# A chunked scan before a mixture of experts: own products head by head, and the decay product in the rows' bank

## The chip, the cores and the metric

The kernel runs on one NeuronCore of a Trainium2 chip. The metric is device time in microseconds: the median of 3 runs is 271.99 us (271.18 to 272.0). One more execution, the profiled one, took 271.81 us; its span, from the first to the last recorded instruction, is 270.0 us. Engines are called PE (TensorE), DVE (VectorE), ACT (ScalarE), POOL (GpSimd) and SP (the queue that issues most DMAs).

## The reference, cut to what matters

Two parts follow each other. The first is a state-space scan (Mamba2 SSD) over 4 batches, 8 heads and 768 steps, with 32 values per head and a state of 16 x 32. It goes chunk by chunk:

```
CB = C_chunk @ B_chunk.T                      # scores of a chunk
y_intra = (CB * L) @ x_chunk                  # L: decay from step j to step i, causal
y_inter = (C_chunk @ state) * decay_to_i      # what came before the chunk
state = decay_full * state + sum_j decay_from_j * outer(B_j, x_j)
```

The second is a top-1 mixture of 8 experts over the 3072 rows of 256 values that the scan makes: a gate product gives 8 logits per row, the row goes to its largest, passes `relu(x @ w1[e]) @ w2[e]` (256 to 1024 to 256) and is scaled by its softmax weight.

## The kernel before

**Tiling of the scan.** The chunk is 64 steps here. The eight heads and two batches of a pair stand side by side: the 128 partitions are two sequences of 64 steps each, a second index `s` holds the other half, and `NT` = 24 chunk pairs (2 pairs of batches, `NC` = 12 chunks each) are walked in order. A loop `for n in range(0, NT + 2)` (L801) is a pipeline written out by hand, three chunks deep: `n` is the chunk whose decays and scores are made, `k = n - 1` the one whose state and output are made, `j = k - 1` the one whose output is turned into rows. All of it stands under a manual schedule: each engine executes its instructions in the order in which the Python code emits them, and the framework adds the semaphore waits between engines. [...]

**One iteration before the change.** `decay(n)` (L355) makes L for all eight heads with one scan on DVE. `fade(k)` (L409) multiplies the carried state by its decay, two ACT instructions, into `Sd`. `own(k)` (L393) forms the chunk's own contribution to the state, B^T x, in PSUM bank A: eight products of two heads of B (32 columns) with two heads of x (64 columns), each in two passes of fp32, so 16 matmuls. A product of two heads with two heads also holds the two cross terms, which aren't wanted. `decay_in` (L329) makes the decay factors of chunk n+2 with three full-size bf16 matmuls into columns 128 to 255 of the same bank A, and ACT copies them to `dec` (L339). `rank_pe` runs in some iterations (below). `state(k)` (L419) adds own products and `Sd`; as the cross terms have to be masked, it takes one DVE instruction per head of the pair, each with the mask column `par[:, u]` as its scalar. `y(k)` (L435) makes the output: first the state products (`ctd` with the carried state S, 32*64 tiles of the array), then the products of M with x (64*32 tiles), into one PSUM tile; ACT copies it to `yT`.

Then come `scores(n)` (L369, the tile `g`, 32*64 tiles), `scaled_B(n)` (L363, on POOL, `bs` = B times L's last column), `decayed_C([n + 2])` (L341, on POOL, `ctd` = C times `dec`), `a_rows(n + 1)` (L348, one bf16 matmul that makes the next scan's input `abc`) and `weigh(n)` (L383, on DVE, M = g times L). ACT has `masks` (the tile `ctm`) in iterations with n mod 4 of 1 or 2, and single jobs at n = 3, 5, 6, 7, 10 and 12. `rows(j)` (L463) turns the output of chunk j into rows of 256 values and 8 logits with two products of 128x136 (four matmuls) in a PSUM bank with the tag "rows", and ACT copies them out (L470). All matmuls of the scan go through the helper `mm` (L175), so the profile shows them with line 176; they are told apart by their tiles. `mm` also counts passes and sends the next loads from SP when a count is reached.

**Routing.** The rows come in groups (`RGS`). When a group is complete, `due` lists three stages for later iterations: stage 0 `choose_max` (maximum, subtraction and comparison, on DVE), stage 1 `choose` (the one-hot row `oh_all`, on DVE, then counts on POOL) and stage 2 `rank_pe` and `rank` (four to six small matmuls, then two DVE instructions that make the position `pos`). Before the change stages 0 and 1 fall into the same iteration for all but the first group, and stage 2 into the one after; the rank's PSUM tile has the tag "rows". After stage 2 each iteration places one chunk's rows in DRAM with an indirect DMA from POOL (L553). At n = 23 the first expert's rows are loaded from DRAM (`a_load`), and the experts follow, with PE products `h_ps` (L685) and `y_ps` (L720).

Of the kernel before, what the change touches and what calls it, by code (L numbers as in the profile page):

```python
# [9 lines left out]
FP32 = mybir.dt.float32  # L10
# [4 lines left out]
ALU = mybir.AluOpType  # L15
# [4 lines left out]
NB, NH, S, D, NS = 4, 8, 768, 32, 16  # L20
N, DM, E, F = 3072, 256, 8, 1024
CH = 64
NP = NB // 2
NC = S // CH
NT = NP * NC
CG = 4
# [3 lines left out]
R0 = [sum(RGS[:i]) for i in range(len(RGS))]  # L30
RG = max(RGS)
# [13 lines left out]
def ssd_then_moe(ctx, tc, x, ad_in, az_in, B, BT, CT, w_gate, w1, w2, out):  # L45
# [16 lines left out]
    def bc(ap, shape):  # L62
        return ap.to_broadcast(shape)
# [17 lines left out]
    azp = [sm.tile([128, 512], BF16, name=f"azp{p}") for p in range(NP)]  # L81
    hsel = sm.tile([128, NC, NH, NS], BF16, name="hsel")
    adp = [sm.tile([128, NP * 128], BF16, name=f"adp{i}") for i in range(3)]
    bs = [sm.tile([128, 8, NS], FP32, name=f"bs{i}") for i in range(2)]

    oh_all = route.tile([128, NT, E], BF16, name="oh_all")
    cnt = route.tile([128, len(RGS) + 2, E], BF16, name="cnt")
# [216 lines left out]
    def decay_ready(p, t):  # L304
        r = slice(2 * p, 2 * p + 2)
        clip(nc.gpsimd, t[:, r])
        nc.gpsimd.tensor_copy(d1[:, r, 0:1], t[:, r, 0:1])
        nc.gpsimd.memset(t[:, r, 0:1], 0.0)
# [14 lines left out]
    def state_bank(k):  # L323

        if "A" not in st[k]:
            st[k]["A"] = ps.tile([128, 2, 128], FP32, name="A", bufs=1)
        return st[k]["A"]

    def decay_in(ns, bank):  # L329
        for i, n in enumerate(ns):  # L330
# [32 lines left out]
    def scaled_B(n):  # L363
        if n % NC == NC - 1:
            return
        nc.gpsimd.tensor_tensor(out=bs[n % 2], in0=gr[n // CG]["B"][:, n % CG].rearrange("p (h m) -> p h m", h=8),  # L366
                                in1=bc(st[n]["L"][:, :, CH - 1:CH], [128, 8, NS]), op=ALU.mult)

    def scores(n):  # L369
        c = n % CG  # L370
# [22 lines left out]
    def own(k):  # L393
        if k % NC == NC - 1:
            return
        A = state_bank(k)
        xk = gr[k // CG]["x"][:, k % CG]

        for s in range(2):
            for t in range(2):  # L400
                for v in range(2):
                    r = slice(64 * t, 64 * t + 64)
                    h = 4 * s + 2 * v
                    mm(A[32 * (2 * t + v):32 * (2 * t + v) + 32, 0, 64 * s:64 * s + 64],
                                     lhsT=bs[k % 2][r, h:h + 2].rearrange("p u m -> p (u m)"),
                                     rhs=xk[r, h * D:(h + 2) * D], start=(s == 0), stop=(s == 1),
                                     skip_group_check=True)

    def fade(k):  # L409

# [8 lines left out]
    def state(k):  # L419
        c = k % NC  # L420
        if c == NC - 1:
            return
        new = wk.tile([128, 2, 2 * D], FP32, name="S", bufs=3)
        A = st[k]["A"][:, 0].rearrange("p (s d) -> p s d", s=2)
        for u in range(2):
            d = slice(D * u, D * u + D)
            if c == 0:
                nc.vector.tensor_scalar(out=new[:, :, d], in0=A[:, :, d], scalar1=par[:, u:u + 1], scalar2=None,
                                        op0=ALU.mult)
            else:  # L430
                nc.vector.scalar_tensor_tensor(out=new[:, :, d], in0=A[:, :, d], scalar=par[:, u:u + 1],  # L431
                                               in1=st[k]["Sd"][:, :, d], op0=ALU.mult, op1=ALU.add)
        carry[k + 1] = new

    def y(k):  # L435
        p = ps.tile([128, 2, 512], FP32, name="y", bufs=1)
        inter = k % NC > 0
        xk = gr[k // CG]["x"][:, k % CG]
        if inter:
            for s in range(2):  # L440
                for t in range(2):
                    for v in range(2):
                        r = slice(64 * t + 32 * v, 64 * t + 32 * v + 32)
                        o = s * CH
                        mm(p[64 * v:64 * v + 64, t, s * CH:s * CH + CH], lhsT=carry[k][r, s],
                                         rhs=st[k]["ctd"][r, o:o + CH], start=(s == 0), stop=False,
                                         skip_group_check=True)
        for s in range(2):
            for q in range(4):
                for t in range(2):  # L450
                    r = slice(64 * t, 64 * t + 64)
                    o = (4 * s + q) * D
                    mm(p[D * q:D * q + D, t, s * CH:s * CH + CH], lhsT=xk[r, o:o + D],
                                     rhs=st[k]["M"][r, 4 * s + q], start=(not inter and s == 0), stop=True,
                                     skip_group_check=True)
        st[k]["yT"] = wk.tile([128, 2, 128], FP32, name="yT")
        nc.scalar.copy(out=st[k]["yT"], in_=p[:, :, 0:128])  # L457

# [1 line left out]
    rt = [(sm if i < GA else route).tile([128, n, W], FP32, name=f"rows{i}") for i, n in enumerate(RGS)]  # L460
    grp = [g for g, n in enumerate(RGS) for _ in range(n)]

    def rows(k, bank):  # L463

        p = ps.tile([128, DM + E], FP32, name="rows_ps", tag=bank, bufs=1)
        for t in range(KT):
            mm(p[:, 128 * t:128 * t + HB], lhsT=st[k]["yT"][:, t], rhs=turn[:, HB * t:HB * t + HB],
                             start=(t == 0), stop=(t == KT - 1), skip_group_check=True)
        g = grp[k]
        nc.scalar.copy(out=rt[g][:, k - R0[g], 0:DM + E], in_=p)  # L470


    def ci(g):
# [2 lines left out]

    rt_v = {}

    def choose_max(g):
        n = RGS[g]  # L480
        lg = rt[g][:, :, 128:HB]
        sh = [128, n, E]
        mx = route.tile([128, RG], FP32, name="mx")[:, 0:n]
        nc.vector.tensor_reduce(mx, lg, axis=AX, op=ALU.max)
        sub = route.tile([128, RG, E], FP32, name="sub")[:, 0:n]
        nc.vector.tensor_tensor(out=sub, in0=lg, in1=bc(mx[:, :, None], sh), op=ALU.subtract)

        eq = route.tile([128, RG, E], FP32, name="eq")[:, 0:n]
        nc.vector.scalar_tensor_tensor(out=eq, in0=sub, scalar=0.0, in1=bc(rev_e[:, None, :], sh),
                                       op0=ALU.is_equal, op1=ALU.mult)  # L490
        rt_v[g] = eq

    def choose(g):
        n = RGS[g]
        sl = slice(R0[g], R0[g] + n)
        eq = rt_v[g]
        m2 = route.tile([128, RG], FP32, name="m2")[:, 0:n]
        nc.vector.tensor_reduce(m2, eq, axis=AX, op=ALU.max)
        nc.vector.tensor_tensor(out=oh_all[:, sl, :], in0=eq, in1=bc(m2[:, :, None], [128, n, E]), op=ALU.is_equal)
# [279 lines left out]
    with tc.manual_schedule():  # L779
# [3 lines left out]
        zero = wake()  # L783
        hs = early_consts()
        nc.gpsimd.memset(d1, 0.0)
        decay_ready(0, adt)
        split_az(0, azt)
        masks(0)
# [12 lines left out]
        for n in range(0, NT + 2):  # L801
# [3 lines left out]
            jobs = due.get(n, [])  # L805
            if n < NT:
                decay(n)
            if 0 <= k < NT:
                fade(k)
                own(k)  # L810
                if n > 1 and n + 2 < NT:
                    decay_in([n + 2], state_bank(k)[:, 1:2])
                for stage, q in jobs:
                    if stage == 2:
                        rank_pe(q, ps.tile([128, RG + 1, E], FP32, name="rank", tag="rows", bufs=1))
                state(k)
                y(k)
            for stage, q in jobs:
                if stage == 0:
                    choose_max(q)  # L820
                if stage == 1:
                    choose(q)
                if stage == 2:
                    rank(q)
                    if q < GA:
                        todo += list(range(R0[q], R0[q] + RGS[q]))
            if n < NT:
                scores(n)
                scaled_B(n)
                if n > 1 and n + 2 < NT:  # L830
                    decayed_C([n + 2])
                if n + 1 < NT:
                    a_rows(n + 1)
                weigh(n)

                if c in (1, 2) and g + 1 < NG:
                    masks(g + 1, (c - 1,))
                if n in act_jobs:
                    act_jobs[n]()
                if n == 12:  # L840
                    empty_consts()
            if 0 <= j < NT:
                if n == NT + 1:
                    keep_on()
                rows(j, "A" if n == NT + 1 else "rows")
                q = grp[j]
                if n == NT + 1:
                    a_xT(0, ps, "abc")
                    next_halves(1)
                if j == R0[q] + RGS[q] - 1:  # L850
                    if q < GA:
                        for i, d in enumerate((1, 2, 3) if q == 0 else (1, 1, 2)):
                            due.setdefault(n + d, []).append((i, q))
                    else:
                        choose_max(q)
                        choose(q)
                        count(q)
            if n == 0:
# [174 lines left out]
```

## Time and profile before

| what | value |
|---|---|
| median of 3 runs | 271.99 us |
| the profiled execution: its time, its span | 271.81 us, 270.0 us |
| PE busy in the span | 252.9 us (94%) |
| DVE, ACT, POOL busy in the span | 110.7, 104.5, 87.0 us |
| granted TensorE clock, mean | 0.992 |
| scan of L: first and last start | 7.1 and 76.8 us |
| first load of rows for an expert issued | 79.07 us |
| first expert product | 83.20 us |

A profile line gives start and duration in microseconds (in the timeline), engine, source line, operation, output tile, input tiles, shape and count; "idle before" names what ended the wait. Consecutive instructions of a kind are merged, and "x16" then stands for 16 matmuls whose durations overlap, since matmuls are pipelined. A matmul's tile of the array is given as rows*columns: 128*128 is the whole array, 64*32 and 32*64 are parts of it that work side by side.

### The profile page before, as it was taken

To read this page: it belongs to the slowest core of one execution; us is meant where nothing else is said; L and a number is where in the kernel's file an instruction comes from. 1 tells how busy PE (TensorE), PEld (TensorE's weight loads), DVE (VectorE), ACT (ScalarE), POOL (GpSimd) and SP (SyncE) were. 2 spreads that over 40 slices of the span, in tenths; PEclk is the share of its full clock that TensorE was granted. 3 is DMA by queue.
4 is the path that set the end of the run, shared out by engine and by line. 5 is a ranking of instruction groups with operands and counts; after the bars stand their busy time and mean duration, and the time that the engine had idled before them with its cause. 6 is when DMAs were issued, how large, how long until landed. Compare 5 with 4: busy or idle time off the path is not lost.

```text
span 270.0 us, 7603 instructions
## 1 busy us (share of the span) xinstructions
PE 252.9 (94%) x3044; PEld 213.7 (79%) x3067; DVE 110.7 (41%) x358; ACT 104.5 (39%) x304; POOL 87.0 (32%) x171
## 2 busy tenths in 40 slices
PE   8799898999997999999999999999999999999990
PEld 2577677677776888888888888888998978989770
DVE  4889887888854240421211111233225115321010
ACT  6958574655543423223232323141050520604200
POOL 5666875866720002025504120202211102121021
PEclk9999999999999999999999999999999999999996
DMA  6956767671434899949695959533330601401010
GB/s 182 374 172 171 228 199 236 165 247 51 135 118 101 212 367 310 384 177 294 236 256 202 279 199 335 130 91 78 103 85 9 94 4 30 90 6 40 2 35 28
DMA packets 29715, 43.57 MB, mean 161 GB/s; under 512 B 16203, under 2 KB 19917, under 8 KB 27984
## 3 DMA queue, kind: packets, MB, share of 16 engines
q1 hardware_dynamic: 27152, 36.32, 45.4%
q0 software_dynamic: 2496, 6.41, 7.1%
q8 instruction: 36, 0.59, 0.9%
q14 instruction: 31, 0.25, 0.3%
HBM read 29.10 MB, written 10.73 MB: 147 GB/s over the span
## 4 chain that ended last, share of the span: by engine, by line
PE 82%; DVE 5%; DMA 4%; issue 4%; POOL 2%; ACT 1%; POOLq 0%; ACTq 0%; DVEq 0%
PE h_ps L685 33%; PE y_ps L720 30%; PE y L176 5%; PE rows_ps L176 4%; PE g L176 3%; PE A L176 3%; PE yh_ps L731 3%; DVE L L359 2%; DMA x_hbm<-rows,pos 1%; DMA xs<-x_hbm 1%; DMA az<-in_az_dram 1%; DMA ct<-in_CT_dram 1%; DVE M L386 1%; PE rank L176 1%; DVE S L431 1%
## 5 line engine op out<-in xcount | busy, mean ns | idle before, releaser
L685 PE MATMUL h_ps<-xT,w 128*128 128x256 f32 (+3 forms) x516 | 90.3, 334 | 0.6 <-ACT xT L641 0.5
L685 PEld LDWEIGHTS h_ps<-xT,w 128*128 128x128 f32 x516 | 81.3, 190 | 8.2 <-ACT xT L641 0.7
L720 PE MATMUL y_ps<-w,hT 128*128 128x256 f32 x384 | 84.9, 380 | 0.0
L720 PEld LDWEIGHTS y_ps<-w,hT 128*128 128x128 f32 x384 | 72.6, 190 | 10.5 <-issue 0.8
L696 ACT ACTIVATE hT<-h_ps 128x256 f32<-128x256 f32 (+3 forms) x128 | 43.3, 339 | 60.8 <-PE h_ps L685 53.1
L711 POOL DMA_INDIRECT out_dram<-yo,xs x24 | 23.7, 988 | 91.1 <-ACT yo L703 64.7
L553 POOL DMA_INDIRECT x_hbm<-rows,pos x24 | 24.4, 1015 | 20.6 <-DMA x_hbm<-zrows 13.3
L359 DVE TENSOR_TENSOR_SCAN L<-abc,ident 128x512 f32<-128x512 f32 x24 | 29.1, 1213 | 0.0
L651 DVE COPY pl<-xs 128x256 uint16<-128x256 uint16 x44 | 10.4, 298 | 43.8 <-DMA xs<-x_hbm 43.7
L658 DVE COPY xT<-plT 128x512 uint16<-128x512 uint16 (+1 forms) x30 | 10.6, 415 | 33.6 <-DMA plT<-pl 27.8
L703 ACT ACTIVATE yo<-y_ps,gate 128x256 f32<-128x256 f32 x14 | 6.6, 474 | 39.4 <-PE y_ps L720 24.5
L386 DVE TENSOR_TENSOR M<-g,L 128x512 f32<-128x512 f32 x24 | 16.5, 687 | 5.6 <-PE g L176 5.1
L176 PE MATMUL rows_ps<-turn,yT 128*128 128x136 f32 x96 | 15.4, 283 | 3.5 <-issue 2.7
L705 DVE TENSOR_SCALAR yo<-y_ps,gate 128x256 f32<-128x256 f32 x10 | 4.8, 482 | 29.3 <-PE y_ps L720 29.3
L176 PE MATMUL g<-ctm,bt 32*64 32x128 f32 x384 | 16.3, 280 | 0.5 <-ACT ctm L293 0.4
L176 PEld LDWEIGHTS rows_ps<-turn,yT 128*128 128x128 f32 x96 | 14.5, 192 | 1.3 <-issue 0.4
L711 POOL DMA_INDIRECT out_dram<-yh,xh x4 | 3.9, 978 | 35.7 <-ACT yh L733 23.9
L470 ACT COPY rows<-rows_ps 128x264 f32<-128x264 f32 x24 | 9.1, 380 | 13.5 <-PE rows_ps L176 10.9
L176 PE MATMUL y<-M,xn 64*32 64x64 f32 x768 | 12.9, 223 | 1.2 <-issue 1.2
L457 ACT COPY yT<-y 128x256 f32<-128x256 f32 x24 | 8.9, 372 | 12.2 <-PE y L176 10.2
L176 PEld LDWEIGHTS g<-ctm,bt 32*64 32x64 f32 x384 | 10.4, 131 | 3.2 <-ACT ctm L293 0.9
L366 POOL TENSOR_TENSOR bs<-bn,L 128x128 f32<-128x128 f32 x22 | 9.0, 410 | 11.1 <-DVE L L359 10.0
(132 smaller groups left out, 203.3 us busy)
## 6 DMA issues: line engine op xcount, KB each, us to landing
w<-in_w_dram SPq DMA_DIRECT2D x13, 1024.0 KB
x_hbm<-zrows SPq DMA_DIRECT2D x8, 463.8 KB
xn<-in_x_dram SPq DMA_DIRECT2D x12, 256.0 KB
w<-in_w_dram SPq DMA_DIRECT2D x12, 256.0 KB
xs<-x_hbm SPq DMA_DIRECT2D x8, 265.0 KB
ct<-in_CT_dram SPq DMA_DIRECT2D x6, 256.0 KB
bt<-in_BT_dram SPq DMA_DIRECT2D x6, 256.0 KB
bn<-in_B_dram SPq DMA_DIRECT2D x6, 256.0 KB
```

The lines of the kernel that those rows point to most:

```text
L176: i = nc.tensor.matmul(out, lhsT=lhsT, rhs=rhs, **kw)
L359: nc.vector.tensor_tensor_scan(out=s["L"].rearrange("p h i -> p (h i)"), data0=s["abc"], data1=ident8.rearrange("p h i -> p (h i)"), initi ...
L366: nc.gpsimd.tensor_tensor(out=bs[n % 2], in0=gr[n // CG]["B"][:, n % CG].rearrange("p (h m) -> p h m", h=8), in1=bc(st[n]["L"][:, :, CH - ...
L386: nc.vector.tensor_tensor(out=s["M"].rearrange("p (s v u) i -> p s v (u i)", s=2, v=2), in0=s["g"][:, :, 0:256].rearrange("p v (s f) -> p ...
L470: nc.scalar.copy(out=rt[g][:, k - R0[g], 0:DM + E], in_=p)
L553: s_ = nc.gpsimd.indirect_dma_start(out=x_hbm[:, :], out_offset=bass.IndirectOffsetOnAxis(ap=pos[:, k:k + 1], axis=0), in_=rt[grp[k]][:, k ...
L651: nc.vector.tensor_copy(pl[:, i, :, t], f[:, :, HB * t:HB * t + 128])
L658: nc.vector.tensor_copy(xT.bitcast(U16).rearrange("p t (j c) -> p c t j", c=2), tt)
L685: nc.tensor.matmul(p[:, i:min(i + step, n)], lhsT=w[:, c:c + 128], rhs=xT[:, t, i:min(i + step, n)], start=(t == 0), stop=(t == KT - 1))
L696: nc.scalar.activation(hT[:, f, 0:n], p, func=ACT.Relu)
L711: s_ = nc.gpsimd.indirect_dma_start(out=out[:, :], out_offset=bass.IndirectOffsetOnAxis(ap=xs[:, TOK:TOK + 1].bitcast(I32), axis=0), in_=y ...
L720: nc.tensor.matmul(p, lhsT=hT[:, f], rhs=w_sb[e][1][:, f * DM:f * DM + DM], start=(f == 0), stop=(f == FT - 1))
```

## The change

The own products are made for one head at a time. `bs` gets four slots per pair of heads, of which the first and last hold the two heads of B and the middle two are zero; a product takes two neighbouring slots as weights, so one head of B stands beside zeros, and the cross terms are zero. There are 16 products of 32 columns instead of eight of 64, in 32 matmuls. `state` then needs no masks and is one DVE instruction over both heads. Two POOL fills at the start set the zeros.

In `y` the products of M with x come first and the state products last. `decay_in` leaves its place after `own` and bank A; it now stands right before `rows`, into columns of the rows' PSUM tile behind the 264 that the rows use, and the rows follow into the same tile. `decayed_C` is issued at the head of the next iteration, for n+1. The rank's matmuls go to bank A, behind the own products' columns, and come after `y`. `choose_max` moves ahead of `fade` and `own`; its subtraction is done by POOL (for the last group by DVE), and the comparison joins `choose`.

```diff
-    bs = [sm.tile([128, 8, NS], FP32, name=f"bs{i}") for i in range(2)]
+    bs = [sm.tile([128, 4, 4, NS], FP32, name=f"bs{i}") for i in range(2)]
...
-            st[k]["A"] = ps.tile([128, 2, 128], FP32, name="A", bufs=1)
+            st[k]["A"] = ps.tile([128, 256], FP32, name="A", bufs=1)
         return st[k]["A"]
+
+    def rank_bank(k):
+        return state_bank(k)[:, 128:128 + (RG + 1) * E].rearrange("p (n e) -> p n e", e=E)
+
+    def rows_bank():
+
+        return ps.tile([128, DM + E + 128], FP32, name="rows_ps", tag="rows", bufs=1)
...
-        nc.gpsimd.tensor_tensor(out=bs[n % 2], in0=gr[n // CG]["B"][:, n % CG].rearrange("p (h m) -> p h m", h=8),
-                                in1=bc(st[n]["L"][:, :, CH - 1:CH], [128, 8, NS]), op=ALU.mult)
+
+        nc.gpsimd.tensor_tensor(out=bs[n % 2][:, :, 0:4:3],
+                                in0=gr[n // CG]["B"][:, n % CG].rearrange("p (w u m) -> p w u m", w=4, u=2),
+                                in1=bc(st[n]["L"][:, :, CH - 1:CH], [128, 8, NS]).rearrange("p (w u) m -> p w u m", u=2),
+                                op=ALU.mult)
...
         for s in range(2):
-            for t in range(2):
-                for v in range(2):
-                    r = slice(64 * t, 64 * t + 64)
-                    h = 4 * s + 2 * v
-                    mm(A[32 * (2 * t + v):32 * (2 * t + v) + 32, 0, 64 * s:64 * s + 64],
-                                     lhsT=bs[k % 2][r, h:h + 2].rearrange("p u m -> p (u m)"),
-                                     rhs=xk[r, h * D:(h + 2) * D], start=(s == 0), stop=(s == 1),
-                                     skip_group_check=True)
+            for u in range(2):
+                for t in range(2):
+                    for v in range(2):
+                        r = slice(64 * t, 64 * t + 64)
+                        o = (4 * s + 2 * v + u) * D
+                        mm(A[32 * (2 * t + v):32 * (2 * t + v) + 32, 64 * s + D * u:64 * s + D * u + D],
+                                         lhsT=bs[k % 2][r, 2 * s + v, 2 * u:2 * u + 2].rearrange("p b m -> p (b m)"),
+                                         rhs=xk[r, o:o + D], start=(s == u == 0), stop=(s == u == 1),
+                                         skip_group_check=True)
...
-        for u in range(2):
-            d = slice(D * u, D * u + D)
-            if c == 0:
-                nc.vector.tensor_scalar(out=new[:, :, d], in0=A[:, :, d], scalar1=par[:, u:u + 1], scalar2=None,
-                                        op0=ALU.mult)
-            else:
-                nc.vector.scalar_tensor_tensor(out=new[:, :, d], in0=A[:, :, d], scalar=par[:, u:u + 1],
-                                               in1=st[k]["Sd"][:, :, d], op0=ALU.mult, op1=ALU.add)
+        A = st[k]["A"][:, 0:128].rearrange("p (s d) -> p s d", s=2)
+        if c == 0:
+            nc.vector.tensor_copy(new, A)
+        else:
+            nc.vector.tensor_tensor(out=new, in0=A, in1=st[k]["Sd"], op=ALU.add)
...
-    def choose_max(g):
+    def choose_max(g, eng=nc.gpsimd):
...
-        nc.vector.tensor_tensor(out=sub, in0=lg, in1=bc(mx[:, :, None], sh), op=ALU.subtract)
...
+        eng.tensor_tensor(out=sub, in0=lg, in1=bc(mx[:, :, None], [128, n, E]), op=ALU.subtract)
+        rt_v[g] = sub
...
+        for t in bs:
+            nc.gpsimd.memset(t, 0.0)
...
             if n < NT:
                 decay(n)
+                if n > 2 and n + 1 < NT:
+                    decayed_C([n + 1])
+            for stage, q in jobs:
+                if stage == 0:
+                    choose_max(q)
             if 0 <= k < NT:
                 fade(k)
                 own(k)
-                if n > 1 and n + 2 < NT:
-                    decay_in([n + 2], state_bank(k)[:, 1:2])
+                state(k)
+                y(k)
                 for stage, q in jobs:
                     if stage == 2:
-                        rank_pe(q, ps.tile([128, RG + 1, E], FP32, name="rank", tag="rows", bufs=1))
-                state(k)
-                y(k)
+                        rank_pe(q, rank_bank(k))
...
-                if n > 1 and n + 2 < NT:
-                    decayed_C([n + 2])
...
+                if n > 1 and n + 2 < NT:
+                    bank = rows_bank()
+                    decay_in([n + 2], bank[:, None, DM + E:])
             if 0 <= j < NT:
                 if n == NT + 1:
                     keep_on()
-                rows(j, "A" if n == NT + 1 else "rows")
+                    bank = ps.tile([128, 512], FP32, name="last_ps", tag="A", bufs=1)
+                rows(j, bank if bank is not None else rows_bank())
```

In `y` the two loops over products change places, as said; the last of them carries the closing flag.

## The prediction

> **What bounds the kernel now.** I read the chain of work that ended last first, then the waits, then the scan in order of time. The chain's page gives 82% of the span to PE, and the two expert products (L685, L720) are 63% of it. The change touches only the scan, so I asked what sets the scan's pace. The timeline of TensorE matmuls over iteration n=21:
>
> ```profile
> 70.94 0.43 PE L176 MATMUL A<-xn,bs 64*32 64x64 f32 x16
> 71.30 0.34 PE L176 MATMUL A<-adp,hsel 128*128 128x128 bf16 x3
> 71.57 0.46 PE L176 MATMUL y<-ctd,S 32*64 32x64 f32 x16
> 71.96 0.45 PE L176 MATMUL y<-M,xn 64*32 64x64 f32 x32
> 72.34 0.67 PE L176 MATMUL g<-ctm,bt 32*64 32x128 f32 x16
> 73.17 0.63 PE L176 MATMUL rows_ps<-turn,yT 128*128 128x136 f32 x4 [0.16 <-issue]
> 73.72 0.43 PE L176 MATMUL A<-xn,bs 64*32 64x64 f32 x16
> ```
>
> Start to start, the groups take 0.36, 0.27, 0.39, 0.38, 0.60 up to the weight load of `selx` at 72.94, 0.23 to the rows and 0.55: 2.78 us, back to back. An iteration with a rank has some 0.29 more. VectorE has 1.21 (scan L) + 0.45 (two S) + 0.69 (M), 2.1 us with overlaps, and some 1.0 more where it chooses. PE therefore sets the pace in 13 of the 19 iterations n=2 to 20 at 2.78, and in 6 at 3.07. That gives 54.6, less 0.36 and 0.39 for the sequence's edge, which has no own products in one iteration and no state products in the next: 53.8. The windows view has 59.99 us from the first to the last of these own products, and PE 54.24 busy. So 6.2 us are lost in pauses of PE and waits for VectorE.
>
> Other instructions of n=21, and a decay copy at 46.57, with what each waited for:
>
> ```profile
> 46.19 0.34 PE L176 MATMUL A<-adp,hsel 128*128 128x128 bf16 x3
> 46.57 0.27 ACT L339 COPY dec<-A 128x128 f32<-128x128 f32 x1 [0.25 <-PE A L176]
> ...
> 71.04 0.38 ACT L470 COPY rows<-rows_ps 128x264 f32<-128x264 f32 x1 [0.92 <-PE rows_ps L176]
> 71.32 0.59 ACT L416 ACTIVATE Sd<-S,dec 128x64 f32<-128x64 f32 x2
> 72.01 0.27 ACT L339 COPY dec<-A 128x128 f32<-128x128 f32 x1
> 72.31 0.47 DVE L431 SCALAR_TENSOR_TENSOR S<-A,par,Sd 128x64 f32<-128x64 f32 x2 [0.20 <-ACT dec L339]
> 72.54 0.37 ACT L457 COPY yT<-y 128x256 f32<-128x256 f32 x1 [0.27 <-PE y L176]
> ```
>
> S reads columns 0 to 127 of bank A, the copy `dec` columns 128 to 255, and S uses nothing of this `dec`. Yet S starts 0.03 after the copy. The waits view has six such waits, 2.8 us: two engines are kept apart by the bank, not by the columns. This is the line that decides my forecast.
>
> [...] the own products' sixteen starts lie within 0.43-0.22=0.21, the next group starts at 0.36, so 0.15 after the last start, against some 0.06 between rounds. [...] no run here has 32 columns.
>
> **The change part by part.**
>
> *Own products.* 8 products of 64 columns in 16 matmuls become 16 of 32 columns in 32. Four tiles work side by side, so four rounds become eight. A round takes about 0.06 for 64 columns (own: 0.21 for four, y's M-products: 0.24) and 0.11 for 128 (scores: 0.67-0.28=0.39 for four). By columns, 32 take 0.03: eight rounds and a lead of 0.03 are 0.27. With a round still at 0.06 it is 0.5; under 0.22 it can't fall, since y's 32 M-products start 0.007 apart (0.24/32). I take 0.27, because the rounds of 64 and 128 columns follow the columns.
>
> *Order on PE.* Own (64*32) is followed by the M-products (64*32), the state products (32*64) by the scores (32*64), abc by decay and rows (all 128*128): three drains go. Own 0.27 (before 0.36), M-products 0.38, state products 0.46-0.22+0.06=0.30 (0.39), scores 0.60, abc 0.23, decay 0.12+0.05=0.17 (0.27), rows 0.55: 2.50, or 0.28 less. M of the iteration before is ready over 1 us early, so the M-products going first cost nothing. With a rank two drains come back (0.19): 0.09 less. Sum: -13x0.28-6x0.09=-4.2 us.
>
> *Decay in the rows' bank.* This adds a wait. The three decay matmuls, ACT's copy `dec` and the rows now use one tile and bank, and the rows write while `dec` would read. By the S wait above, the rows must wait for the copy. From the first decay matmul: 0.34 to the end, 0.04 to ACT's start (46.53 to 46.57), 0.27 copy, 0.04 back to PE. The last is in the chain in order of time, between the copy `xT` and the first h:
>
> ```profile
> 82.78 0.38 ACT xT L641
> 83.16 0.04 issue
> 83.20 11.68 PE h_ps L685 x56
> ```
>
> And four rows that had to wait took 0.73 at 60.55 against 0.63, so 0.10 for weights not loaded ahead. Together 0.79 where 0.17 would do: +0.62. Behind the waiting rows in PE's queue stand the next own products and everything after them. Over 19 iterations: +11.8. Bounds: 0.4 if a part overlaps, 0.7.
>
> *What ACT does first.* `dec` stands behind `yT` and the mask (ctm, 0.72) where there is one. `yT` ends 0.96 after the state products start, a mask at 1.66; decay's matmuls end at 0.30+0.60+0.23+0.34=1.47. So a mask adds 0.15, in nine iterations: 1.4. ACT's jobs at n=3, 5, 6, 7, 10 and 12 (casts of 0.40 and 0.62, `zrows` 1.08) add 0.1+0.4+0.4+0.5+0.4+0.5=2.3. Today these hide beside PE.
>
> *Rank in bank A.* It no longer needs the rows' bank, but must wait for S to have read A, with the scores queued behind. S waits for Sd, which ends 0.97 after own starts (70.94 to 71.90); S takes 0.33 (0.274 for 64 columns; M's slope, (687-274)/448, is 0.92 ns per column), ends at 1.35, rank starts at 1.40. PE would be there at 0.27+0.38+0.39=1.04. +0.35 in six iterations: 2.1. If S comes earlier, nothing.
>
> *VectorE and POOL.* One S for two saves 0.12 of VectorE per iteration; the subtraction moved to POOL saves 0.2 to 0.5 in six, less the return wait. On POOL it takes 0.24 (between 0.20 for 8 columns and 0.32 for 64), `bs` is behind it and needed over 2 us later; `bs` into steps I leave at 0.41. `ctd` moves to the next iteration's head, still ahead of its use by more than an iteration. All lies beside PE: zero; if PE weren't the bound, it would give some 3 us. Two fills of 128x256 at 0.32 meet 0.45 idle POOL at 3.64: 0.19 late, with the scan of `adf` at 6.62 far behind. Loads sent by the count of PE passes go out in fewer iterations, which is no later.
>
> *Sum.* PE's floor is 53.8-4.2+11.8+1.4+2.3+2.1=67.2. Of the 6.2 above the floor I keep 1.5, as waits for VectorE vanish and PE's pauses fall partly into its new waits: 68.7 against 59.99, +8.7. From the last own to the next scores it is 0.96 instead of 1.40: -0.45. The last placements follow the scan, which follows the scores; their landing (79.06) and the load of xs (82.04) start the experts, which PE fills without a wait for loads. So +8.2 passes through: 271.81+8.2=280.0 for the profiled execution (span 270.0). The median of the runs, 271.99, is 0.2 from it; I predict 280.0.
>
> **Rivals.** (1) *The rows don't wait for the copy*: what is kept apart is only what shares columns. For it: no row of the trace shows PE held by a copy of other columns; against it: the six S waits[...]. Then 53.8-4.2+2.1, pauses of 3.4, 1.5 for VectorE in five choosing iterations: 56.6, so -3.4-0.45: 268.0, faster. The deciding point is a turn-around under 0.28 per iteration, which the copy of 0.27 alone nearly fills. (2) *The wait is there, but small*: 0.52 (weights loaded ahead), no rank stall, no pauses left: 53.8-4.2+9.9+1.4+1.5=62.4, +2.4-0.45: 273.8. For it: PE lost 6.2 us before in places that the wait may cover. (3) *Own rounds don't shrink with the columns*: +0.23 in 17 more iterations on my case: 284. For it: the weights' loads double in number; against: eight-wide rounds of M-products issue one pair each 7 ns.
>
> **How the numbers follow.** My case 0.65 (276 to 284), rival 1 0.13, rival 2 0.13 (270 to 276, of which 0.03 under the bound of faster and 0.04 within it), rival 3 0.09 (to 288). 0.3% is about what a measurement of this kernel can tell from no change. Faster 0.16, same 0.04, slower 0.80. The range 271.5 to 286 leaves out rival 1 and the end of rival 3.
>
> **What would show it.** Right: rows starting some 0.05 after each `dec` copy with ACT `dec` as releaser, PE idle 0.5 to 0.7 there, iterations of 3.1 us where they were 2.8, S without waits for `dec`, six ranks released by S. Wrong: rows within 0.2 of the decay's start (rival 1), own over 0.45 to its next group (rival 3), or VectorE still ending the waits of the scores. The prediction fails if the copy runs before PE gets to it, or if PE's pauses shrink by more than I gave.

## The result and the profile after

The changed kernel takes 289.35 us (median of four executions, 283.27 to 305.51), beside 272.0 us (271.18 to 272.35) for the kernel before on the same chip. The ratio is 1.0475, with a 95% interval of 1.0372 to 1.0578; like every ratio below it leaves out executions in which TensorE had a lower granted clock for longer (here two of the four, with 0.974 and 0.891 in the mean, beside 0.990 and 0.991 in the other two), so the lines below are of a later execution of the same kernel, in which it had not. The ratio puts the kernel at 284.9 us. A later set has 286.71 us (284.26 to 287.71) against 268.78: 1.0629 (1.0554 to 1.0703). The profiled execution of it took 287.71 us, its span is 286.0 us. I forecast 280.0, slower, and 271.5 to 286 as the range. It is slower, by more than I said: 284.9 lies near the upper end of the range, and the later set just above it.

From the page of the kernel after, the span, and the shares of the engines in the chain of work that ended last ("issue" is time in which an engine waited for nothing that the profile shows):

```profile
span 286.0 us, 8312 instructions
...
PE 80%; ACT 9%; issue 6%; DVE 1%; DMA 1%; POOL 1%; ACTq 0%; POOLq 0%
```

ACT has 9% of the chain, where it had 1% before, and "issue" 6%, where it had 4%. The loss lies in the scan: from the first to the last start of the scan of L it is 69.7 us before and 86.1 us after, 16.4 more, while the span grew by 16.0. The timeline of an iteration of the kernel after in which PE doesn't pause (n=21, with the decay and rows ahead of it; start, duration, what):

```profile
85.60 0.33 PE L176 MATMUL rows_ps<-adp,hsel 128*128 128x128 bf16 x3 [0.16 <-issue]
86.05 0.27 ACT L346 COPY dec<-rows_ps 128x128 f32<-128x128 f32 x1 [1.33 <-PE rows_ps L176]
...
86.36 0.73 PE L176 MATMUL rows_ps<-turn,yT 128*128 128x136 f32 x4 [0.43 <-ACT dec L346]
...
87.03 0.46 PE L176 MATMUL A<-xn,bs 64*32 64x32 f32 x32
...
87.30 0.53 PE L176 MATMUL y<-M,xn 64*32 64x64 f32 x32
87.41 0.59 ACT L426 ACTIVATE Sd<-S,dec 128x64 f32<-128x64 f32 x2
...
88.03 0.29 DVE L438 TENSOR_TENSOR S<-A,Sd 128x128 f32<-128x128 f32 x1 [0.69 <-ACT Sd L426]
...
88.82 0.33 PE L176 MATMUL rows_ps<-adp,hsel 128*128 128x128 bf16 x3 [0.16 <-ACT yT L463]
```

The rows start 0.04 us after the copy `dec` has ended and 0.76 after the first decay matmul, and they take 0.73 instead of 0.63. From the own products to the next group it is 0.27. S waits for `Sd`, no longer for `dec`. From decay to decay it is 3.22 us, where an iteration took 2.78 before. The waits of PE's matmuls from 7 to 95 us (total, times, longest):

```profile
PE rows_ps L176 <- ACT dec L346: 10.2, 20, 1.0
PE y L176 <- issue: 4.0, 5, 1.3
...
PE A L176 <- issue: 1.6, 1, 1.6
...
PE g L176 <- issue: 0.9, 1, 0.9
```

The first line is the wait that I forecast, in every iteration that has a decay product. The other three are not: seven pauses, 6.5 us, in which PE waited for nothing that the profile shows. The kernel before had only 1.4 us of this, in four pauses, all in y (the short stop of 0.16 to 0.3 us ahead of a group of rows or decay products, also marked issue, is left out in both). From 7 to 85 us of it:

```profile
PE y L176 <- issue: 1.4, 4, 0.5
```

Two of the new pauses in the timeline of PE:

```profile
45.17 0.37 PE L176 MATMUL y<-M,xn 64*32 64x64 f32 x13
46.80 0.41 PE L176 MATMUL y<-M,xn 64*32 64x64 f32 x19 [1.26 <-issue]
...
56.41 0.45 PE L176 MATMUL A<-xn,bs 64*32 64x32 f32 x31
58.46 0.21 PE L176 MATMUL A<-xn,bs 64*32 64x32 f32 x1 [1.60 <-issue]
```

Each is in the middle of a group of like matmuls; nothing in the profile holds it up. The pauses come at fixed places in PE's own instruction list. Counting PE's records (loads of weights and matmuls) from the start, and putting beside each the packet of 16384 bytes that came before it on the queue whose kind the profile gives as "instruction" (39 packets, 0.64 MB in the span; six of the seven pauses; times in us):

```
after, record   PE goes on at   packet began, took    PE goes on after its end
 958             22.68           19.73, 1.50           1.45
2232             46.80           43.14, 2.44           1.22
2741             58.46           56.15, 1.02           1.29
2996             63.45           61.11, 0.96           1.38
3251             67.46           64.59, 1.44           1.43
3506             73.14           70.75, 0.88           1.51
```

The distances are 5 x 254.8, 2 x 254.5, 255, 255 and 255 records. Over all kept profiles, every pause of this kind during the scan that lasted over 0.5 us ended 1.2 to 1.6 us after the end of such a packet; the two longer ones of the kernel before (0.42 and 0.49) did not. In the kernel before, 14 such packets begin from 12.78 us to just before 74.88, and 3478 of PE's records start in that time: 248 to a packet, about the distance of the pauses. After the last of the six pauses the clock goes too. The windows view of the kernel after (window, PE busy, PEld, DVE, ACT, POOL, granted clock, DMA share, GB/s):

```profile
72.00:74.00 2.00, 0.91 (x13) 0.47 (x9) 0.44 (x2) 0.14 (x1) 1.02 (x1) 1.00 0.00 0
74.00:76.00 2.00, 1.57 (x51) 1.25 (x53) 1.45 (x2) 0.71 (x3) 0.86 (x2) 0.70 0.22 76
76.00:78.00 2.00, 2.00 (x72) 1.64 (x59) 0.29 (x1) 0.94 (x4) 1.01 (x1) 0.50 0.18 66
78.00:80.00 2.00, 1.39 (x33) 1.00 (x33) 1.73 (x2) 0.81 (x3) 0.45 (x1) 0.94 0.01 2
```

PE was busy for less than half of the first window, and then had half its clock: 0.6 + 1.0 + 0.1 = 1.7 us of full clock lost. Such a window isn't enough for it: from 56 to 58 PE was busy for 0.86, and the clock stayed at 1.00. Before the change the clock was 1.00 from 11 to 73 us.

### The profile page after: what moved, and what is told of

It is laid out like the page before. It is cut to its first block, busy times and chain, and to the rows that moved or that the text cites. A ratio compares the mean times of both kernels' runs of the same rounds, so it can differ in the third digit from the quotient of the medians.

```text
span 290.6 us, 8335 instructions
## 1 busy us (share of the span) xinstructions
PE 261.4 (90%) x3419; PEld 216.6 (75%) x3419; DVE 107.8 (37%) x330; ACT 105.5 (36%) x304; POOL 89.4 (31%) x179
## 4 chain that ended last, share of the span: by engine, by line
PE 79%; ACT 6%; DMA 5%; issue 4%; DVE 3%; POOL 1%; SPq 0%; POOLq 0%; ACTq 0%; DVEq 0%
PE h_ps L688 31%; PE y_ps L723 27%; PE rows_ps L176 7%; PE y L176 4%; PE g L176 3%; PE A L176 3%; PE yh_ps L734 2%; ACT dec L346 2%; PE abc L176 2%; DMA x_hbm<-rows,pos 2%; DMA xn<-in_x_dram 1%; DMA xs<-x_hbm 1%; DMA az<-in_az_dram 1%; ACT Sd L426 1%; DVE L L366 1%
## 5 line engine op out<-in xcount | busy, mean ns | idle before, releaser
L176 PE MATMUL rows_ps<-turn,yT 128*128 128x136 f32 x92 | 18.0, 319 | 12.7 <-ACT dec L346 12.2
L176 PEld LDWEIGHTS rows_ps<-turn,yT 128*128 128x128 f32 x92 | 13.1, 201 | 16.0 <-ACT dec L346 15.8
L176 PE MATMUL g<-ctm,bt 32*64 32x128 f32 x384 | 18.4, 289 | 1.1 <-issue 0.9
L176 PE MATMUL y<-M,xn 64*32 64x64 f32 x768 | 15.1, 232 | 2.7 <-issue 2.6
L176 PEld LDWEIGHTS g<-ctm,bt 32*64 32x64 f32 x384 | 12.1, 138 | 2.7 <-ACT ctm L293 1.2
L176 PEld LDWEIGHTS y<-M,xn 64*32 64x32 f32 x768 | 10.5, 108 | 4.8 <-issue 4.6
```

The lines of the kernel that those rows point to most:

```text
L176: i = nc.tensor.matmul(out, lhsT=lhsT, rhs=rhs, **kw)
```

## The experiments

The theory at the start was my forecast's: the copy `dec` holds up the rows (the *wait theory*). Its rival was that the pauses of PE grow as well (the *pause theory*). A *drain*, in the forecast and the expectations, is the gap where the form of PE's tiles changes: in n=21 of the kernel before it is 0.15 us from the last start of a group to the first of the next, at each of the four changes from own to the scores, and in an iteration of the kernel after (own at 90.27 us of its first profile) it is 0.01 from own to the products of M, which have the same form. Each result is given beside the kernel before on the same chip: 268.78 us for the first four, 271.74 for the next four, 270.46 for the last.

**The decay product behind the rows.** The changed kernel, with the three matmuls emitted behind the rows' four, in the same bank, and then both copies:

```diff
-                    bank = rows_bank()
-                    decay_in([n + 2], bank[:, None, DM + E:])
+                    bank = rows_bank()
...
+        if nxt is not None:
+            decay_mm([nxt], p[:, None, DM + E:])
         nc.scalar.copy(out=rt[g][:, k - R0[g], 0:DM + E], in_=p[:, 0:DM + E])
+        if nxt is not None:
+            decay_copy([nxt], p[:, None, DM + E:])
```

> The changed kernel, but the three decay matmuls are issued behind the rows' matmuls into the same bank, and the two copies follow; nothing is left out. Wait theory: TensorE no longer waits for the decay's copy, rows follow abc within 0.25, and 12 us or more go: 268 to 273. Pause theory: the wait mattered little by itself, pauses remain, 278 to 283. If the wait was only standing where another wait stands next (the rank's or the state's): above 278 with a new releaser in the rows' place.

Measured: 280.4 us, 1.0413 (1.035 to 1.0477); the changed kernel itself, in the same set, 286.71. Only 6.3 us come back, which the pause theory's range holds. The rows' wait for `dec` is gone from the profile, and PE's waits from 7 to 90 us begin with

```profile
PE y L176 <- issue: 6.4, 7, 1.7
```

So the wait theory alone fails: in place of the wait PE meets longer pauses. In this profile the granted clock also fell to half four times during the scan, and each time 1.7 us of full clock were lost, 6.8 in all, where the changed kernel lost 1.7.

> The changed kernel once more. Wait theory (the rows stand behind the copy of the decay, 20 waits, 12.2 us of TensorE's idle time in its profile): about 285, 1.048 of before. Pause theory (TensorE pauses longer because the own products doubled its instructions there): the same time, with pauses of TensorE inside the products of M of over 3 us in total. Clock theory: some executions show a granted clock under 0.98 and are over 290.

Measured: the 286.71 us told above.

**The decay part alone.** The kernel before, with `decay_in` ahead of the rows in the rows' bank and `decayed_C` at the next head:

```diff
-                    decay_in([n + 2], state_bank(k)[:, 1:2])
...
-                rows(j, "A" if n == NT + 1 else "rows")
+                p = ps.tile([128, DM + E + 128], FP32, name="rows_ps", tag="A" if n == NT + 1 else "rows", bufs=1)
+                if n > 1 and n + 2 < NT:
+                    decay_in([n + 2], p[:, None, DM + E:])
+                rows(j, p)
```

> The kernel before, with one part of the change alone: the decay matmuls stand right ahead of the rows in the rows' bank, and ctd moves to the next iteration's head; own products, state, output order, rank and choice as before. Wait theory: 0.60 of wait in each of 20 iterations less one drain of 0.1, and 3 to 4 us for what stands ahead in ACT's queue: 282 to 286. If the cost comes from the other parts (pause theory): 272 to 277.

Measured: 283.27 us, 1.053 (1.048 to 1.0579): 14.5 us more. No PE instruction was added. PE's waits from 7 to 92 us begin with

```profile
PE rows_ps L176 <- ACT dec L339: 10.7, 20, 1.1
```

So the wait is real, and has the size forecast. Not all of the 14.5 us is its own, though: the clock was at half for a stretch of the scan (columns as above).

```profile
34.00:36.00 2.00, 1.89 (x73) 1.48 (x69) 0.75 (x4) 1.09 (x4) 1.17 (x4) 0.80 0.47 170
36.00:38.00 2.00, 1.26 (x16) 0.72 (x9) 1.33 (x2) 0.30 (x2) 0.99 (x2) 0.50 0.19 68
...
40.00:42.00 2.00, 2.00 (x64) 1.38 (x58) 0.48 (x2) 0.91 (x3) 0.90 (x1) 0.50 0.66 192
```

From 34 to 42 us this is 0.4 + 3 x 1.0 = 3.4 us of full clock, which the kernel before did not lose.

**All but the waits.** The first experiment, with the copy `dec` moved behind the next fade, `decayed_C` behind `scaled_B`, and the rank behind the scores:

```diff
                 fade(k)
+                if late_dec:
+                    decay_copy(*late_dec.pop())
...
+                for stage, q in jobs:
+                    if stage == 2:
+                        rank_pe(q, rank_bank(k))
                 weigh(n)
```

> As the run with the decay behind the rows; besides, the decay's copy is issued behind the next fade, ctd behind bs, and the rank's matmuls stand behind abc, ahead of the rows, with its two DVE instructions behind M; nothing is left out. Wait theory: the drains saved (0.28 in each of 19 iterations, no more given back by the rank) come out: 265 to 269, faster than before. Pause theory: the doubled own products eat them, 270 to 274.

Measured: 281.21 us, 1.0466 (1.0399 to 1.0532). Both theories missed. Taking out more waits gained nothing: PE's pauses at issue in y, A and g grew to 10.0 us. Among the records before which PE paused are 703, 958, 1213, 1468, 2232, 2997 and 4016, all 255 or a multiple of it apart. This is where the third theory came from: what is left is the fetching of PE's instructions (the *fetch theory*), and what counts is their number: PE would pause every 255 records or so where the next packet of 16384 bytes comes late, and 32 more instructions in an iteration would bring these places closer. It is a guess from the places of the pauses and the packets, and its ranges below are estimates of mine. An iteration has 176 PE instructions before the change: 32 for own, 64 + 32 for y, 32 for the scores, 2 for abc, 6 for the decay, 8 for the rows. The own products head by head make it 208.

**Own products whole.** The changed kernel with 16 own matmuls, the compact `bs` and the two masked additions; the wait stays:

```diff
-                        mm(A[32 * (2 * t + v):32 * (2 * t + v) + 32, 64 * s + D * u:64 * s + D * u + D],
-                                         lhsT=bs[k % 2][r, 2 * s + v, 2 * u:2 * u + 2].rearrange("p b m -> p (b m)"),
+                    mm(A[32 * (2 * t + v):32 * (2 * t + v) + 32, 64 * s:64 * s + 64],
+                                     lhsT=bs[k % 2][r, h:h + 2].rearrange("p u m -> p (u m)"),
```

> The changed kernel with its own products whole again (eight of 64 columns, bs dense, two masked additions); the wait of the rows for the decay's copy stays. Fetch theory [...]: pauses at those places fall to what the kernel before has, 278 to 282 against 286.7. If own products cost nothing: 285 to 288.

Measured: 284.85 us, 1.0409 (1.0355 to 1.0463), against 1.0629 for the changed kernel in its set. The intervals do not meet, so the split costs some 2%, as the fetch theory says in sign; the time itself lies between the two ranges expected.

**Own part alone.** The kernel before with only the split own products and the single addition (the same edit, the other way round):

> The kernel before with one part alone: own products head by head beside zeros, and one state addition. Fetch theory: 208 instructions of TensorE in an iteration where there were 176[...]: 274 to 280. By the busy time of TensorE alone: 269 to 271, no more than 2 us over the kernel before.

Measured: 278.72 us, 1.0215 (1.0162 to 1.0269). The fetch theory's range holds it. My forecast has this part as a gain; it is a loss of some 6 us by the ratio, 7 by the medians. In its trace own takes 0.38 to the decay's matmuls (35.81 to 36.19), where it took 0.36, so the products themselves account for some 0.4 of it (0.02 in each of 19 iterations). The pauses at issue come to 3.6 us (1.4 before), and a stretch at half clock from 49 to 53 lost 1.7.

**Idle instructions.** The test of the number itself: the kernel before, with 16 more matmuls of one column, on zeros, behind the own products, into columns of bank A that nobody reads. This is 32 more PE instructions in an iteration, as the split adds, and next to no other work:

```diff
+        for i in range(4):
+            for t in range(2):
+                for v in range(2):
+                    o = 32 * (2 * t + v)
+                    r = slice(64 * t, 64 * t + 64)
+                    nc.tensor.matmul(A[o:o + 32, 2, i:i + 1], lhsT=zero[r, 0:32], rhs=zero[r, 0:1], start=True, stop=True,
```

> The kernel before with 16 one-column bf16 matmuls on zeros behind its own products, into columns that nobody reads: 32 instructions more per iteration, and next to no work (16 starts of 7 ns are 0.11 us, 2.4 us in 22 iterations). Fetch theory: as the own part alone, 274 to 280[...]. If it is the products' work: 269 to 272.

Measured: 283.01 us (280.02 to 285.66), 1.0426 (1.0323 to 1.0528), 11.3 us more by the medians. The profiled execution took 280.02 us, 8.3 more. Timeline of PE in an iteration of it, and its waits from 7 to 85 us:

```profile
28.40 0.43 PE L176 MATMUL A<-xn,bs 64*32 64x64 f32 x16
28.65 0.26 PE L414 MATMUL A<-wake 64*32 64x1 bf16 x16
28.84 0.34 PE L176 MATMUL A<-adp,hsel 128*128 128x128 bf16 x3
```

```profile
PE y L176 <- issue: 3.6, 7, 1.0
PE g L176 <- issue: 1.5, 2, 0.8
```

From own to decay it is 0.44 where it was 0.36. Some 0.08 in each of 19 iterations is 1.5 us. The pauses at issue are 5.1 us, 3.7 more than before, and a stretch at half clock from 60 to 64 lost 1.7. So of the 8.3 us of this execution 1.5 are the matmuls' own time, and 5.4 are pauses and clock. The count of PE instructions thus has a price of its own. That the fetch is what charges it is the reading that fits the places of the pauses and the packets ahead of them; it isn't shown, as no run here makes the fetch itself faster.

**No wait, own whole.** All but the waits, with the own products whole:

> The kernel that had the decay behind the rows and the rank behind abc, with its own products whole again; nothing is left out. Fetch theory: [...] 264 to 268, faster than the kernel before. If the order of the products, or the place of ctd and of the rank, is what costs: 276 to 281, as with the own products head by head.

Measured: 278.95 us, 1.0313 (1.0234 to 1.0392). The fetch theory's range missed, and the other range (276 to 281: the order of the products, or the places of `decayed_C` and the rank, cost the time) holds it. With 176 instructions the pauses remain, 7.4 us of them. One lasted 1.41 us up to 63.86, and the windows after it (columns as above) show what followed:

```profile
62.00:64.00 2.00, 0.59 (x21) 0.40 (x25) 0.35 (x2) 0.99 (x2) 1.08 (x4) 1.00 0.28 101
64.00:66.00 2.00, 2.00 (x25) 1.56 (x23) 1.39 (x4) 0.00 (x0) 0.00 (x0) 0.72 0.01 5
66.00:68.00 2.00, 1.96 (x53) 1.30 (x50) 0.97 (x3) 1.02 (x4) 1.61 (x3) 0.50 0.07 23
```

The clock came back between 70 and 72 (0.57 there). One reading is that an iteration without waits is so short that even 176 instructions are needed faster than they come; it isn't shown, and the places remain a rival.

**Rows first, own whole.** The first experiment with the own products whole; rank and `decayed_C` stay where the change has them:

> The changed kernel with the decay's matmuls issued behind the rows' matmuls in the same bank, and with the own products whole again (16 matmuls, the two masked state additions): 176 PE instructions in an iteration instead of 208. Fetch theory [...]: the iteration without waits is still shorter than the fetches allow, so the pauses stay: 274 to 279 us. Rival (the late time of the version with every wait moved came of where it put the rank and the decay's product): less than 272 us, below the kernel before.

Measured: 273.83 us, 1.0161 (1.0104 to 1.0217), just under the fetch theory's range and above the rival's. Against 1.0313 for the version before it, with intervals that don't meet, the places do cost some 1.5%; whether by way of the pauses isn't shown. From the first to the last scan of L it is 70.0 us, against 69.7 before. The rest comes at the scan's end; PE's waits from 7 to 92 us:

```profile
PE y L176 <- issue: 4.7, 4, 3.0
PE A L176 <- DVE S L444: 2.2, 4, 0.6
```

A single pause of 3.0 us stands before record 4013, behind the last scan, and the scan's last products run at half clock (0.50 from 82 to 84). The packet ahead of the pause began only at 78.5, 7.1 us after the one before; why so late is not known. The rank's wait for S costs 2.2 here.

**The choice part alone.** The kernel before with `choose_max` ahead of the fade, the subtraction on POOL and the comparison in `choose`:

```diff
-        nc.vector.tensor_tensor(out=sub, in0=lg, in1=bc(mx[:, :, None], sh), op=ALU.subtract)
+        eng.tensor_tensor(out=sub, in0=lg, in1=bc(mx[:, :, None], [128, n, E]), op=ALU.subtract)
```

> The kernel before with the choice's part of the change alone: subtraction on POOL ahead of the fade, comparison on DVE behind it. No PE instruction is added. If DVE and the choice lie off the path that sets the end: within 1 us of the kernel before. Rival (POOL's subtraction delays the fade and b's product behind it, and with them g): 2 to 4 us slower.

Measured: 270.3 us, 1.001 (0.9977 to 1.0043): no difference, as the forecast's "zero" for VectorE and POOL says.

**A candidate to beat both.** The kernel before with the choice part, and the decay product behind the rows with its copy after the next fade. A drain and the wait of S go, no PE instruction is added:

> The kernel before with the choice's part, and with the decay's matmuls behind the rows' matmuls in the rows' bank, copied out by ACT behind the next fade: one drain of PE and the wait of the state's matmuls for the decay's copy go, no PE instruction is added. Wait theory (each microsecond of wait that goes on PE is won): 266 to 270 us. Fetch theory (the time won is spent waiting for instructions): 270 to 274 us.

Measured: 273.4 us, 1.0113 (1.0023 to 1.0202). Not faster. The fetch theory's range holds it, but it does not tell the theories apart, since it has a wait of its own that I hadn't thought of: the rank's tile also has the tag "rows", and so waits until the copy has left that bank. From PE's waits in its profiled execution (275.96 us):

```profile
PE rank L176 <- ACT dec L341: 4.2, 5, 0.9
```

**Weights behind the scan.** The version without waits and with own whole, with the loads of the experts' weights sent when the scan is done:

```diff
-        order = later_groups[2] + later_groups[3] + later_groups[4] + later_groups[5] + w_loads(0) + w_loads(1)[0:4]
+        order = later_groups[2] + later_groups[3] + later_groups[4] + later_groups[5]
```

> The version with every wait moved and the own products whole, with the loads of the experts' weights sent behind the scan instead of during it. If the traffic of these loads makes the fetches of PE's instructions late: the fetch packets take at most 1.1 us, the pauses shrink, and the scan ends 2 us or more sooner than in the version with the loads in it. If not: the scan takes as long. The whole time says little, as the weights come late either way.

Measured: 281.1 us, in a single execution. From the first to the last scan of L it is 69.2 us, against 75.8 with the loads inside: 6.6 less. But the fetch packets took 0.93 to 1.62 us, no less than in the version with the loads (mean 1.23 against 1.18), and y and the scores have twelve pauses at issue up to 92 us. So it isn't shown that the traffic makes fetches slow. What differs is that the clock stayed at 1.00 to the scan's end, where the version with the loads inside lost 3.4 us of full clock; that is at most half of the 6.6. Whether the traffic or chance decides on it, one execution can't say.

**Side by side.** For the main versions, from their profiles: PE instructions in an iteration, the rows' wait for `dec`, the pauses at issue in y, A and g (7 to 90 us), the full clock lost by the end of the scan (us), and the ratio to the kernel before.

| version | instructions | wait for `dec` | pauses | clock lost | ratio |
|---|---|---|---|---|---|
| before | 176 | none | 1.4 | 0 | 1 |
| the change | 208 | 10.2 | 5.8 | 1.7 | 1.0629 |
| decay part alone | 176 | 10.7 | 0.0 | 3.4 | 1.053 |
| own products whole | 176 | 11.9 | 0.6 | 6.8 | 1.0409 |
| own part alone | 208 | none | 3.6 | 1.7 | 1.0215 |
| idle instructions | 208 | none | 5.1 | 1.7 | 1.0426 |
| decay behind the rows | 208 | none | 7.5 | 6.8 | 1.0413 |
| all but the waits | 208 | none | 10.0 | 3.4 | 1.0466 |
| no wait, own whole | 176 | none | 7.4 | 3.4 | 1.0313 |
| rows first, own whole | 176 | none | 5.0 | 3.4 | 1.0161 |

The profile of "own products whole" is of an execution of 288.07 us, with more time at half clock than its ratio has, so its pauses may be fewer than they would be at full clock. With 176 instructions and the wait the pauses all but vanish. With 208 they are 3.6 us or more, with the wait or without, and in the short iterations of the last two versions they come with 176 as well. The half clock does not need them: the decay part lost 3.4 us of full clock with no pause.

## Why the prediction was right or wrong

The sign was right, and the wait that decided the forecast is there. The size was short: the first ratio gives 12.9 us more, the later set 17.9, where I had 8.2. That 284.9 still lies inside the range is partly luck, since its upper end was drawn for rival 3, which did not happen, and not for what did.

**Decay in the rows' bank: right.** +0.62 in each iteration was forecast. In the undisturbed iteration the rows start 0.76 after the decay, where 0.17 would do, and take 0.10 longer, which my 0.79 already held: 0.69. The part alone cost 14.5 us, where wait and ACT's work ahead of it had been put at 11.8 + 3.7 = 15.5. That the two sums are so close is partly chance, as up to 3.4 of the 14.5 are the stretch at half clock, which I had not forecast. Rival 1, that the rows don't wait, and rival 2, that the wait is small, are out.

**What ACT does first: half of it.** I had 1.4 for masks and 2.3 for jobs. Of the 19 iterations, 15 have 0.69 to 0.76 and four (n=5, 7, 10 and 12) 1.09 to 1.31: 5.0 - 4 x 0.75 = 2.0 us in all.

**Own products: the duration right, the gain wrong.** 0.27 is what I forecast, so rival 3 is out. 32 products in 0.27 are some 0.008 us apart, on four tiles side by side. The part alone still lost some 6 us, and idle instructions in the same number 8.3 in the profiled execution: it is what the split adds to PE's instruction list, and no step of mine priced that.

**Order on PE: nearly right.** The undisturbed iteration takes 3.22 from own to own, and I had 3.12, wait included. The M-products take 0.46 instead of 0.38, and the state products 0.17 instead of 0.30 up to the scores. In the whole time the gain doesn't show: all versions with the new order of y's products are slower than the kernel before.

**Rank in bank A: right in size.** In the six iterations it is 0.79 to 1.12 from the state products to the scores, against 0.17: 4.8 us, where I had 2.1 for S, 1.1 for two drains and 1.7 for the rank itself, 4.9. Only two of the six are shown as released by S.

**VectorE and POOL: right for the choice**, by its part alone. The single addition of S was measured only together with the split.

**"Of the 6.2 above the floor I keep 1.5, as waits for VectorE vanish and PE's pauses fall partly into its new waits": this step failed.** I took PE's pauses for slack that new waits would swallow, and gave the split's 32 further instructions nothing. With the measured iteration the floor of 67.2 becomes 67.2 + 19 x 0.10 - 1.7 = 67.4. From the first own products to those of iteration 21 it took 75.7 us. So 8.3 lie above the floor, where I kept 1.5. 5.8 of them are pauses at issue; the rest, some 2.5 us, is the stretch at half clock and single waits for POOL, ACT and DVE. That is 6.8 us more than I kept, and takes 280.0 to 286.8; the profiled execution took 287.71. The idea of the step was not wrong everywhere: in the decay part alone, with 176 instructions, the wait did swallow the pauses (0.0 left). It is with 208 that they outlast it.

The same gap kept me from seeing that the change would not win even without the wait: the two versions with the split and without the wait took 280.4 and 281.21 us. In all the profiles of this study no two instruction packets during the scan start less than 3.34 us apart, and their mean in the kernel before is 4.44. If 3.34 us were a limit for 255 instructions, the distance of the pauses, 208 would allow no iteration under 208/255 x 3.34 = 2.72, about the 2.78 that the kernel before took, whatever the drains give, and the gain of the order on PE, 0.28 in an iteration, would be spent by the split before it was made. This is an estimate from the smallest spacing and the distance of the pauses; that it is a limit isn't shown. With 176 instructions it would allow 2.31, so it doesn't explain the pauses of the versions without waits that have 176.

What stays open: why some packets begin late, whether the fetch itself is what PE waits for, and what would keep a short iteration with 176 instructions from pausing, since both versions of that kind with the weights' loads in their place, 273.83 and 278.95 us, were slower than the kernel before.

## What to carry to other kernels

Where PE runs small matmuls back to back, count its instructions as well as its columns: a product cut in two for a tidier result can cost more by its further instructions (here some 6 us for 32 in an iteration) than it frees elsewhere. A PSUM tile into which PE writes, from which ACT copies, and into which PE writes again cost PE the whole turn-around in every iteration here, even at disjoint columns (10.7 us in 20 iterations); put the second product ahead of the first reader, or in another bank (in two banks, as in the kernel before, the rows had no such wait). And a pause of an engine that the profile puts down to nothing isn't simply slack: find its place in the instruction list, and ask whether the change brings the engine to such places faster, before counting on a wait to swallow it.

## What was not expected of the hardware

- Pauses of PE of 0.5 to 3.0 us, some 255 records or a multiple of it apart, that end 1.2 to 1.6 us after the end of a 16 KiB packet on the instruction queue. 32 idle instructions in an iteration cost 8.3 us in the profiled execution, of which some 1.5 are their own time.
- A granted clock of 0.5 in the scan without a long stop of PE. In the kernel after and in the version with own whole and no waits it follows a stretch with PE busy under half of 2 us (0.91 and 0.59); with the idle instructions PE was busy for 1.35 of the 2 us before it, and other stretches under half were followed by no fall. By the windows, a stretch lost 1.7 us of full clock or a multiple of it (kernel after 0.60 + 1.00 + 0.12), so at half clock it lasted some 3.4 us, or a multiple. No pause just before it in the two first named was longer than 1.41 us, though others lay close by. What sets it off isn't shown.
- Taking a wait of 10.2 us from PE gave back 6.3 us: the pauses rose from 5.8 to 7.5 us, and the full clock lost from 1.7 to 6.8.
